# Linear attention and mixture of depths: key transposes in the state banks, a bank for the score row, and wider score compares

## The chip, the cores and the metric

The kernel runs on one core of one Trainium2 chip. The metric is device time in microseconds (us); the kernel before takes 194.52 us, the median of three runs. The engines of a core are PE (TensorE, the matrix engine; its weight loads are listed as PEld), DVE (VectorE), ACT (ScalarE), POOL (GpSimd) and SP (SyncE, used here for loads). The matrix engine writes to PSUM, which has eight banks per partition of 512 float32 values each.

## The reference

Two stages follow each other. The first is a block-wise linear attention with decay over 4 batches, 8 heads, 768 positions and head size 64, in blocks of 64:

```python
intra = einsum(einsum(qb, kb) * Dmask, vb)          # inside the block
inter = einsum(qb * lam_pow, kv_state)              # from the state
out[:, :, sl] = intra + inter
kv_state = lam_block * kv_state + einsum(kb * rev_pow, vb)
```

The second is a mixture of depths on the result x, reshaped to (4, 768, 512). A score x @ w_gate is taken for every token, the 128 tokens of a batch with the highest scores are chosen, and only these go through a two-layer network:

```python
xe = x[b, top_idx]
ye = maximum(xe @ w1, 0) @ w2                       # 512 -> 1024 -> 512
out[b, top_idx] = xe + sigmoid(score)[:, None] * ye
```

## The kernel before

A group g is 128 positions of one batch for all heads, that is two blocks of 64; there are NT = 6 groups per batch and NG = 24 in all. The main loop takes one step per group. The order of instructions on every engine is the order in which the program is written: nothing is reordered by a scheduler, and each engine works its instructions off in that order, waiting where an operand or a buffer isn't ready. The framework places the waits.

**PSUM.** Two output tiles `po` (two banks each) hold scores and outputs of a group. Two banks `pu` (one per block) hold the key-value products of a group, in their lower 256 columns. Two more banks, handed out in turn by `bank()`, serve everything else: the transposed queries `tp_qT` and keys `tp_kT`, and for the expert `pt` (its transposed input), `ph` (hidden layer), `py` (output) and `pk` (chosen tokens). While the expert holds a bank for `ph` or `py`, all others share the remaining one.

**A step g.** The steps of attention overlap: in step g, `from_scores(g)` (line 282) and `outputs(g)` finish group g; `scores(g+1)` (line 217), `from_states(g+1)` (line 271) and `masked(g+1)` (line 224, on DVE, writes `p`) work on the next one; `state_products(g+2)` (line 240) fills `pu`, and `next_state` (lines 259 and 261, on DVE) adds it to the state that `decay_state` (line 250, on POOL) has scaled. There are two states per group, and so two such pairs per step. `transposes(g+2)` brings queries and keys into the form that the matmuls need (line 195 on PE, copies in line 199 on ACT), `queries_decayed(g+2)` (line 204) and `keys_decayed(g+3)` (line 184) scale them on POOL. `gate_scores(g)` (line 306, on DVE) yields the score of each token.

**Choosing tokens.** `row(g-1)` transposes the scores of a group so that every partition has them in a row (line 326): it writes them into columns 256 to 383 of `pu[0]`, and ACT copies them to `sc_row` (line 329). `compare(g-1)` counts on DVE how many tokens beat each token: ties within the group (line 339), earlier groups against the new row, one instruction for each (line 345), and the new group against all so far (line 350). Both `pu` readers of a score row must be done before the next step's state products may use the bank. After a batch's last group `ranks` sums the counts, and `hit` (line 368) marks the token of each rank.

**The expert.** `plan(b)` lays its pieces out over the following steps. With s the first step after batch b: ranks run at the end of step s, `tokens` (line 379) early in step s+1, `fetch` gathers the rows from the output in memory with an indirect DMA (line 402, issued by POOL) at the start of step s+2, and `gate` (transposes of the gathered rows in line 412, and the gate's value) comes in step s+3 behind the attention's state products. Then follow 8 `hidden` pieces (line 440) and 8 `back` pieces (line 454), two or three per step, and a scatter (line 466). The last batch's expert and most of the one before run after the loop.

Of the kernel before, what the change touches and what calls it, by code (L numbers as in the profile page):

```python
# [8 lines left out]
FP32 = mybir.dt.float32  # L9
BF16 = mybir.dt.bfloat16  # L10
# [7 lines left out]
def kernel(  # L18
# [18 lines left out]
    L = 128  # L37
# [125 lines left out]
    def bank(shape, name, hold=False):  # L163

        tag = next(t for t in banks if t not in held)
        banks.remove(tag)
        banks.append(tag)
        if hold:
            held.append(tag)
        return ps_m.tile(shape, FP32, name=name, tag=tag)  # L170
# [17 lines left out]
        )  # L188
        kds[g] = kd

    def transposes(g, name, keep):
        t = loaded[g][0 if name == "qT" else 1]
        tp = bank([128, NHP, L], "tp_" + name)
        for hp in range(NHP):
            nc.tensor.transpose(  # L195
                tp[:, hp, :], in_=t[:, 2 * hp : 2 * hp + 2, :], identity=ident[:]
            )
        dst = att.tile([128, NHP, L], FP32, name=name)
        nc.scalar.copy(out=dst[:], in_=tp[:])  # L199
        keep[g] = dst  # L200

    def queries_decayed(g):
        qs = att.tile([128, NHP, L], FP32, name="qs")
# [27 lines left out]
    def start_u(g):  # L231
        us[g] = [ps_u.tile([128, 512], FP32, name=f"pu{c}") for c in range(2)]
# [80 lines left out]

        return out[0 : b + 1].flatten_outer_dims()

    rows_, beatens, toks, pbs = {}, {}, {}, {}

    def row(g, u, i=0):

        b, t = divmod(g, NT)  # L320
        if t == 0:
            rows_[b] = mod.tile([128, S], FP32, name="sc_row", tag="sc_row")
            beatens[b] = mod.tile([128, NT, NT + 1], FP32, name="beaten")
            nc.gpsimd.memset(beatens[b][:], 0.0)
        pb = us.pop(u)[i][:, 256 : 256 + L]
        nc.tensor.transpose(
            pb, in_=scs[b][:, t : t + 1].broadcast_to([128, 128]), identity=ident[:]
        )
        nc.scalar.copy(out=rows_[b][:, t * L : (t + 1) * L], in_=pb)  # L329
        pbs[g] = pb  # L330

    def compare(g):
        b, t = divmod(g, NT)
        sc, pb, beaten = scs[b], pbs.pop(g), beatens[b]
        cmp = mod.tile([128, S], BF16, name="cmp")
        nc.vector.scalar_tensor_tensor(  # L339
            out=cmp[:, :L], in0=pb, scalar=sc[:, t : t + 1], in1=not_before[:],  # L340
            op0=ALU.is_equal, op1=ALU.mult, accum_out=beaten[:, t, NT : NT + 1],
        )
        for n in range(t):
            cmp = mod.tile([128, S], BF16, name="cmp")
            nc.vector.tensor_scalar(  # L345
                out=cmp[:, :L], in0=pb, scalar1=sc[:, n : n + 1], scalar2=None,
                op0=ALU.is_gt, op1=ALU.add, accum_out=beaten[:, n, t : t + 1],
            )
        cmp = mod.tile([128, S], BF16, name="cmp")
        nc.vector.tensor_scalar(  # L350
            out=cmp[:, : (t + 1) * L], in0=rows_[b][:, : (t + 1) * L],
            scalar1=sc[:, t : t + 1], scalar2=None, op0=ALU.is_ge, op1=ALU.add,
            accum_out=beaten[:, t, t : t + 1],
        )

    def places(b):


        hits = []

        def ranks():
            rank = mod.tile([128, NT], FP32, name="rank")
            nc.vector.tensor_reduce(
                out=rank[:], in_=beatens[b][:], axis=mybir.AxisListType.X, op=ALU.add
            )
            for i in range(NGR):
                hit = mod.tile([128, NT, 128], BF16, name="hit")
                nc.vector.tensor_tensor(
                    out=hit[:], in0=rank[:].unsqueeze(2).broadcast_to([128, NT, 128]),
                    in1=token[:, i * 128 : (i + 1) * 128].unsqueeze(1).broadcast_to([128, NT, 128]),  # L370
                    op=ALU.is_equal,
                )
                hits.append(hit)

        def tokens():
            pk = bank([128, NGR, 2], "pk")
            for i in range(NGR):
                for t in range(NT):
                    nc.tensor.matmul(
                        pk[:, i, :], lhsT=hits[i][:, t, :], rhs=ids[:, b * NT + t, :],  # L380
                        start=(t == 0), stop=(t == NT - 1),
                    )
# [91 lines left out]

    early, gates, later, ranked = {}, {}, {}, {}
    busy_until = [0]

    def put(step, key, piece):  # L480
        later.setdefault(step, []).append((key, piece))

    def in_order(pieces):
        for _, piece in sorted(pieces, key=lambda kp: kp[0]):
            piece()

    def plan(b):
        last = b == B - 1
        s = (b + 1) * NT
        ranks, tokens = places(b)  # L490
        if last:

            def last_row():
                start_u(NG + 2)
                row(NG - 1, NG + 2, 1)
                compare(NG - 1)
                ranks()

            put(s, 35, last_row)
            put(s, 85, tokens)  # L500
        else:
            ranked[s] = ranks
            put(s + 1, 5, tokens)
        for i in range(NGR):
            s = max(s, busy_until[0])
            fetch, gate, pieces = expert(b, i)
            if s + 3 >= NG:
                s = max(s, NG)
                put(s, 86, fetch)
                put(s + 1, 0, gate)  # L510
                for j, piece in enumerate(pieces):
                    put(s + 2, j, piece)
                busy_until[0] = s + 3
                continue
            early.setdefault(s + 2, []).append(fetch)
            gates[s + 3] = gate

            whole = s + 9 <= NG
            counts = [2, 3, 3, 3, 3, 2] if whole else [1, 1, 2]
            assert len(pieces) == 16  # L520
            where = [(s + 3 + i, 10 * (j + 1)) for i, n in enumerate(counts) for j in range(n)]
            where = [w for w in where if w[0] < NG]
            where += [(NG, 10 * (j + 1)) for j in range(len(pieces) - len(where))]
            for (step, key), piece in zip(where, pieces):
                put(step, key, piece)
            busy_until[0] = s + 6 if whole else NG

    keys_decayed(0)
    transposes(0, "qT", qTs)
    transposes(0, "kT", kTs)  # L530
    queries_decayed(0)
    keys_decayed(1)
    start_u(0)
    state_products(0)
    next_state(0)
    decay_state(1)
# [1 line left out]
    decay_state(2)  # L538
    for g in range(3, AHEAD):
        load(g)  # L540
    transposes(1, "qT", qTs)
    transposes(1, "kT", kTs)
    queries_decayed(1)
    keys_decayed(2)
    scores(0)
    from_states(0)
    start_u(1)
    state_products(1)
    masked(0)
    next_state(2)  # L550
# [4 lines left out]
    for g in range(NG):  # L555
        if g + AHEAD < NG:
            load(g + AHEAD)
        if 0 <= g - NT + 2 < n_w:
            load_weights(g - NT + 2)
        if g + 2 < NG:  # L560
            decay_state(2 * g + 4)
        for piece in early.pop(g, []):
            piece()
        from_scores(g)
        outputs(g)
        if g + 1 < NG:
            scores(g + 1)
            from_states(g + 1)
            masked(g + 1)
        start_u(g + 2)  # L570
        if g + 2 < NG:
            state_products(g + 2)
            next_state(2 * g + 4)
            decay_state(2 * g + 5)
        gate_scores(g)
        if g + 2 < NG:
            next_state(2 * g + 5)
        pieces = later.pop(g, [])
        starts = g in gates
        if starts:  # L580
            gates.pop(g)()
        if g + 2 < NG:
            transposes(g + 2, "qT", qTs)
            queries_decayed(g + 2)
        if g + 3 < NG:
            keys_decayed(g + 3)
        if starts and g > 0:
            row(g - 1, g + 2)
            compare(g - 1)
        in_order(pieces)  # L590
        if g + 2 < NG:
            transposes(g + 2, "kT", kTs)
        if not starts and g > 0 and NGR:
            row(g - 1, g + 2)
            compare(g - 1)
        if g in ranked:
            ranked.pop(g)()
        if g % NT == NT - 1 and NGR:
            plan(g // NT)
# [35 lines left out]
```

## Time and profile before

| | |
|---|---|
| device time, median of 3 | 194.52 us |
| profiled execution, span | 192.9 us |
| PE busy | 157.5 us, 82% |
| DVE busy | 104.0 us, 54% |
| POOL busy | 98.9 us, 51% |
| ACT busy | 66.1 us, 34% |
| DMA traffic | 32.26 MB, of which the 16 engines are nine tenths busy until about 116 us |
| copies of qT and kT (ACT) | 24 of 584 ns, 24 of 587 ns |
| compares of line 345 (DVE) | 60, 17.8 us in all |
| gathers of expert rows | 4, of 3.4 to 6.5 us from issue to landing |

A busy share is a mean over the whole span. The program has stretches with different limits: a start, eight steps with attention alone, then steps in which the expert's matmuls fill the matrix engine, and an end with the expert alone. A line of the timeline begins with start and duration in us, then engine, source line, operation, output and inputs, sizes and count; in brackets follows how long the engine was idle before and what ended that. "issue" in such a bracket means that the profile shows no releasing instruction.

### The profile page before, as it was taken

The page shows a single profiled execution, that of the slowest core. Times are in us where ns is not written, and L with a number is a line of the kernel's source. Part 1 is how long each engine was busy: PE and PEld are TensorE (multiplying, and loading weights), DVE is VectorE, ACT ScalarE, POOL GpSimd, SP SyncE. Part 2 cuts the span into 40 slices and gives each one's busy share as a digit, 9 for nine tenths or more (in the row PEclk, how much of TensorE's full clock was granted, in tenths as well). Part 3 has the DMA queues.
Part 4 walks back from the last instruction along what each step waited for, and adds up shares of the span by engine and source line. Part 5 has one row for each costly group of instructions (what it writes and reads, how often), then busy time and mean ns, then how long its engine had stood idle before and what let it go on. Part 6 is the DMA issues. An engine that isn't in the chain of part 4 may idle for free.

```text
span 192.9 us, 8120 instructions
## 1 busy us (share of the span) xinstructions
PE 157.5 (82%) x3520; PEld 125.3 (65%) x3520; DVE 104.0 (54%) x393; ACT 66.1 (34%) x161; POOL 98.9 (51%) x110
## 2 busy tenths in 40 slices
PE   0896776969777399998888899989699899979980
PEld 0675665757666399896646689876467689439630
DVE  4824353667884653448664564754927678730010
ACT  2234333544443224533314353444234352111100
POOL 3486777476858641773556846458197410130002
PEclk9999998899999859999999999999999999999999
DMA  4999999998999999998999993110103211011001
GB/s 104 221 225 268 230 226 256 223 259 187 254 297 287 302 252 259 271 286 233 232 259 259 250 251 112 59 49 11 58 17 99 109 61 54 0 54 54 3 0 56
DMA packets 80964, 32.26 MB, mean 167 GB/s; under 512 B 75680, under 2 KB 75680, under 8 KB 80928
## 3 DMA queue, kind: packets, MB, share of 16 engines
q1 hardware_dynamic: 76688, 23.34, 54.2%
q10 hardware_dynamic: 3600, 6.30, 8.9%
q0 software_dynamic: 640, 2.10, 3.1%
q8 instruction: 28, 0.46, 0.9%
q14 instruction: 8, 0.07, 0.1%
HBM read 24.38 MB, written 7.34 MB: 164 GB/s over the span
## 4 chain that ended last, share of the span: by engine, by line
PE 51%; issue 16%; DVE 10%; POOL 9%; DMA 7%; ACT 4%; POOLq 1%; SPq 0%; ACTq 0%
PE ph L440 12%; PE py L454 11%; PE pu L240 5%; PE po L217 5%; PE po L271 5%; PE tp_qT L195 4%; PE tp_kT L195 4%; POOL qs L204 4%; DMA xs<-out_dram,tok 3%; PE po L282 3%; POOL kd L184 3%; POOL decayed L250 3%; DMA kn<-in_k_dram 3%; ACT kT L199 2%; DVE cmp L345 2%
## 5 line engine op out<-in xcount | busy, mean ns | idle before, releaser
L250 POOL TENSOR_TENSOR decayed<-state,decay 128x256 f32<-128x256 f32 x40 | 35.4, 884 | 39.0 <-DVE state L261 31.6
L204 POOL TENSOR_TENSOR qs<-qT,qpow 128x512 f32<-128x512 f32 x24 | 30.5, 1269 | 14.4 <-ACT qT L199 8.9
L440 PE MATMUL ph<-xsT,w_sb 128*128 128x128 f32 x256 | 32.6, 286 | 0.9 <-ACT xsT L416 0.7
L440 PEld LDWEIGHTS ph<-xsT,w_sb 128*128 128x128 f32 x256 | 31.2, 200 | 1.7 <-ACT xsT L416 1.5
L199 ACT COPY qT<-tp_qT 128x512 f32<-128x512 f32 x24 | 14.0, 584 | 50.0 <-PE tp_qT L195 46.8
L454 PE MATMUL py<-w_sb,hs 128*128 128x512 f32 x64 | 29.2, 596 | 0.0
L224 DVE TENSOR_TENSOR p<-po,mask 128x512 f32<-128x512 f32 x24 | 16.5, 689 | 19.2 <-PE po L271 19.2
L184 POOL TENSOR_TENSOR kd<-kn,kpow 128x512 f32<-128x512 f32 x24 | 25.1, 1044 | 3.2 <-DMA kn<-in_k_dram 3.1
L261 DVE TENSOR_TENSOR state<-pu,decayed 128x256 f32<-128x256 f32 x40 | 16.8, 421 | 16.9 <-POOL decayed L250 16.3
L240 PE MATMUL pu<-vn,kd 64*64 64x64 f32 x704 | 19.7, 229 | 7.3 <-issue 5.2
L240 PEld LDWEIGHTS pu<-vn,kd 64*64 64x64 f32 x704 | 16.1, 140 | 10.1 <-issue 7.0
L217 PE MATMUL po<-qT,kT 64*64 64x64 f32 x768 | 18.3, 228 | 5.0 <-issue 4.5
L271 PE MATMUL po<-state,qs 64*64 64x64 f32 x704 | 17.3, 225 | 5.9 <-POOL qs L204 3.0
L199 ACT COPY kT<-tp_kT 128x512 f32<-128x512 f32 x24 | 14.1, 587 | 23.3 <-PE tp_kT L195 23.3
L195 PE MATMUL tp_qT<-ident,qn 128*128 128x128 f32 x96 | 17.4, 309 | 5.1 <-DMA qn<-in_q_dram 5.1
L339 DVE SCALAR_TENSOR_TENSOR cmp<-pu,sc,not_before 128x128 bf16<-128x128 f32 x24 | 8.4, 349 | 23.8 <-ACT sc_row L329 17.0
L217 PEld LDWEIGHTS po<-qT,kT 64*64 64x64 f32 x768 | 14.5, 137 | 8.1 <-issue 5.4
L271 PEld LDWEIGHTS po<-state,qs 64*64 64x64 f32 x704 | 14.5, 138 | 7.1 <-POOL qs L204 3.7
L454 PEld LDWEIGHTS py<-w_sb,hs 128*128 128x128 f32 x64 | 11.5, 190 | 11.0 <-issue 11.0
L345 DVE TENSOR_SCALAR_CACHE_REDUCE cmp<-pu,sc 128x128 bf16<-128x128 f32 x60 | 17.8, 347 | 0.0
L298 ACT COPY x_b<-po 64x256 f32<-64x256 f32 x48 | 17.6, 366 | 0.6
L282 PE MATMUL po<-vn,p 64*64 64x64 f32 x768 | 16.8, 224 | 0.3 <-DVE p L224 0.3
(55 smaller groups left out, 170.6 us busy)
## 6 DMA issues: line engine op xcount, KB each, us to landing
qn<-in_q_dram SPq DMA_DIRECT2D x24, 256.0 KB, 5.3
kn<-in_k_dram SPq DMA_DIRECT2D x24, 256.0 KB, 5.5
vn<-in_v_dram SPq DMA_DIRECT2D x24, 256.0 KB, 6.0
out_dram<-x_b ACTq DMA_DIRECT2D x24, 256.0 KB, 3.6
w_sb<-in_moe_w_dram SPq DMA_DIRECT2D x8, 512.0 KB, 5.9
wg_b<-in_moe_w_gate_dram SPq DMA_DIRECT2D x1, 256.0 KB
xs<-out_dram,tok POOLq DMA_INDIRECT x4, 4.3
out_dram<-y,tok POOLq DMA_INDIRECT x4, 3.1
```

The costliest lines, as they stand in the source:

```text
L184: nc.gpsimd.tensor_tensor(out=kd[:], in0=loaded[g][1][:], in1=kpow[:].rearrange("p a b -> p (a b)").unsqueeze(2).broadcast_to([128, H, D]) ...
L195: nc.tensor.transpose(tp[:, hp, :], in_=t[:, 2 * hp : 2 * hp + 2, :], identity=ident[:])
L199: nc.scalar.copy(out=dst[:], in_=tp[:])
L204: nc.gpsimd.tensor_tensor(out=qs[:], in0=qTs[g][:], in1=qpow[:].rearrange("p a c i -> p a (c i)"), op=ALU.mult)
L217: nc.tensor.matmul(po[half[c], hh, 1, hp, :], lhsT=kT[half[hh], hp, half[c]], rhs=qT[half[hh], hp, half[c]], start=True, stop=True, skip_g ...
L240: nc.tensor.matmul(us[g][c][half[hh], hp * D : (hp + 1) * D], lhsT=kd[half[c], h, :], rhs=vn[half[c], h, :], start=True, stop=True, skip_g ...
L250: nc.gpsimd.tensor_tensor(out=t[:], in0=states[n][:], in1=decay[:], op=ALU.mult)
L271: nc.tensor.matmul(pos[g][half[hh ^ c], hh, 0, hp, :], lhsT=qs[half[hh], hp, half[c]], rhs=states[n][half[hh], hp, :], start=(hp == 0), st ...
L282: nc.tensor.matmul(pos[g][half[hh ^ c], hh, 0, hp, :], lhsT=p[half[c], hh, hp, :], rhs=vn[half[c], 2 * hp + hh, :], start=(hp == 0 and (2 ...
L345: nc.vector.tensor_scalar(out=cmp[:, :L], in0=pb, scalar1=sc[:, n : n + 1], scalar2=None, op0=ALU.is_gt, op1=ALU.add, accum_out=beaten[:, ...
L440: nc.tensor.matmul(ph[:, fc % 4, :], lhsT=w1_sb[:, dc, fc * 128 : (fc + 1) * 128], rhs=keep["xsT"][:, dc, :], start=(dc == 0), stop=(dc == ...
L454: nc.tensor.matmul(py[:], lhsT=keep["hs"][:, fc, :], rhs=w2_sb[:, fc, :], start=(fc == 0), stop=(fc == NFC - 1),)
```

## The change

The change does four things.

1. The transposed keys are written into columns 256 to 511 of the two `pu` banks, two head pairs in each, and copied out by two ACT instructions in place of one. Both transposes of a group now stand together, ahead of `next_state`, and only the queries take one of the two shared banks.
2. The score row takes a shared bank of its own (`pb`) and leaves `pu`.
3. Older groups are compared with newer ones for two or three groups at a time, from the copied row in SBUF.
4. The order is changed: in the start `queries_decayed(0)` comes ahead of `keys_decayed(0)`; `keys_decayed(g+3)` moves to the front of the step; `gate` moves ahead of the transposes; ranks run one step later; tokens and the gather move to the end of step s+2, while `gate` stays in step s+3; the pieces of the third expert start with one each in the last three steps; the last two rows of the loop come together in step NG-2.

It is meant to free the shared banks and the state banks earlier, and to take waits for compares and ranks away from the matrix engine.

```diff
-    def transposes(g, name, keep):
-        t = loaded[g][0 if name == "qT" else 1]
-        tp = bank([128, NHP, L], "tp_" + name)
...
+    def transposes(g):
+        tq = bank([128, NHP, L], "tq")
+        tk = [u[:, NHP * D :].rearrange("p (a i) -> p a i", i=L) for u in us[g]]
...
+        nc.scalar.copy(out=qT[:], in_=tq[:])
+        kT = att.tile([128, NHP, L], FP32, name="kT")
+        for i in range(2):
+            nc.scalar.copy(out=kT[:, i * W : (i + 1) * W, :], in_=tk[i])
...
-        pb = us.pop(u)[i][:, 256 : 256 + L]
+        pb = bank([128, L], "pb")
...
+    def count_later(b, groups, last):
+        for t in groups:
+            if upto[b][t] < last:
+                cols = slice((upto[b][t] + 1) * L, (last + 1) * L)
+                count(b, t, cols, ALU.is_gt, last)
+                upto[b][t] = last
...
     def compare(g):
-        for n in range(t):
-            cmp = mod.tile([128, S], BF16, name="cmp")
-            nc.vector.tensor_scalar(
-                out=cmp[:, :L], in0=pb, scalar1=sc[:, n : n + 1], scalar2=None,
-                op0=ALU.is_gt, op1=ALU.add, accum_out=beaten[:, n, t : t + 1],
-            )
...
+        count(b, t, slice(0, (t + 1) * L), ALU.is_ge, t)
+        if t == NT // 2 - 1 or (b == B - 1 and t == NT - 2):
+            count_later(b, range(t), t)
+        elif t == NT - 2:
+            count_later(b, range(NT // 3), t)
+        elif t == NT - 1:
+            count_later(b, range(NT // 3, NT - 2), t)
...
         def ranks():
+            count_later(b, range(NT), NT - 1)
...
-            ranked[s] = ranks
-            put(s + 1, 5, tokens)
+            ranked[s + 1] = ranks
+            put(s + 2, 15, tokens)
...
-            early.setdefault(s + 2, []).append(fetch)
+            put(s + 2, 16, fetch)
...
-            counts = [2, 3, 3, 3, 3, 2] if whole else [1, 1, 2]
+            counts = [2, 3, 3, 3, 3, 2] if whole else [1, 1, 1]
...
+    start_u(0)
+    transposes(0)
+    queries_decayed(0)
     keys_decayed(0)
-    transposes(0, "qT", qTs)
-    transposes(0, "kT", kTs)
-    queries_decayed(0)
     keys_decayed(1)
-    start_u(0)
...
-        for piece in early.pop(g, []):
-            piece()
+        if g + 3 < NG:
+            keys_decayed(g + 3)
...
             state_products(g + 2)
+        if g in gates:
+            gates.pop(g)()
+        if g + 2 < NG:
+            transposes(g + 2)
             next_state(2 * g + 4)
             decay_state(2 * g + 5)
...
+        for r in {NG - 2: [g - 1, g], NG - 1: []}.get(g, [g - 1]):
+            if r >= 0 and NGR:
+                row(r)
+                compare(r)
```

More of the change, by code (lines that the diff above doesn't have):

```diff
@@ L189, in keys_decayed @@
         kds[g] = kd
-    def transposes(g, name, keep):
-        t = loaded[g][0 if name == "qT" else 1]
-        tp = bank([128, NHP, L], "tp_" + name)
-        for hp in range(NHP):
-            nc.tensor.transpose(
-                tp[:, hp, :], in_=t[:, 2 * hp : 2 * hp + 2, :], identity=ident[:]
-            )
-        dst = att.tile([128, NHP, L], FP32, name=name)
-        nc.scalar.copy(out=dst[:], in_=tp[:])
-        keep[g] = dst
+    def transposes(g):
+        tq = bank([128, NHP, L], "tq")
+        tk = [u[:, NHP * D :].rearrange("p (a i) -> p a i", i=L) for u in us[g]]
+        W = NHP // 2
+        for i, dst in ((0, tq), (1, None)):
+            for hp in range(NHP):
+                nc.tensor.transpose(
+                    dst[:, hp, :] if i == 0 else tk[hp // W][:, hp % W, :],
+                    in_=loaded[g][i][:, 2 * hp : 2 * hp + 2, :], identity=ident[:],
+                )
+        qT = att.tile([128, NHP, L], FP32, name="qT")
+        nc.scalar.copy(out=qT[:], in_=tq[:])
+        kT = att.tile([128, NHP, L], FP32, name="kT")
+        for i in range(2):
+            nc.scalar.copy(out=kT[:, i * W : (i + 1) * W, :], in_=tk[i])
+        qTs[g], kTs[g] = qT, kT
     def queries_decayed(g):
@@ L314, in rows_upto, with row @@
         return out[0 : b + 1].flatten_outer_dims()
-    rows_, beatens, toks, pbs = {}, {}, {}, {}
-    def row(g, u, i=0):
+    rows_, beatens, toks, upto = {}, {}, {}, {}
+    def row(g):
         b, t = divmod(g, NT)
@@ L324, in row @@
             nc.gpsimd.memset(beatens[b][:], 0.0)
-        pb = us.pop(u)[i][:, 256 : 256 + L]
+            upto[b] = list(range(NT))
+        pb = bank([128, L], "pb")
         nc.tensor.transpose(
-            pb, in_=scs[b][:, t : t + 1].broadcast_to([128, 128]), identity=ident[:]
+            pb[:], in_=scs[b][:, t : t + 1].broadcast_to([128, 128]), identity=ident[:]
         )
-        nc.scalar.copy(out=rows_[b][:, t * L : (t + 1) * L], in_=pb)
-        pbs[g] = pb
+        nc.scalar.copy(out=rows_[b][:, t * L : (t + 1) * L], in_=pb[:])
@@ new lines, in row, with count @@
+        cmp = mod.tile([128, S], BF16, name="cmp")
+        nc.vector.scalar_tensor_tensor(
+            out=cmp[:, :L], in0=pb[:], scalar=scs[b][:, t : t + 1], in1=not_before[:],
+            op0=ALU.is_equal, op1=ALU.mult, accum_out=beatens[b][:, t, NT : NT + 1],
+        )
+    def count(b, t, cols, op, at):
+        cmp = mod.tile([128, S], BF16, name="cmp")
+        nc.vector.tensor_scalar(
+            out=cmp[:, : cols.stop - cols.start], in0=rows_[b][:, cols],
+            scalar1=scs[b][:, t : t + 1], scalar2=None, op0=op, op1=ALU.add,
+            accum_out=beatens[b][:, t, at : at + 1],
+        )
@@ L335, in compare @@
+    def count_later(b, groups, last):
[4 more added lines that the diff above has]
+                upto[b][t] = last
     def compare(g):
         b, t = divmod(g, NT)
-        sc, pb, beaten = scs[b], pbs.pop(g), beatens[b]
-        cmp = mod.tile([128, S], BF16, name="cmp")
[L339 to L342, printed above, removed]
@@ L343, in compare @@
-        for n in range(t):
-            cmp = mod.tile([128, S], BF16, name="cmp")
-            nc.vector.tensor_scalar(
-                out=cmp[:, :L], in0=pb, scalar1=sc[:, n : n + 1], scalar2=None,
-                op0=ALU.is_gt, op1=ALU.add, accum_out=beaten[:, n, t : t + 1],
[L348 to L354, printed above, removed]
+        count(b, t, slice(0, (t + 1) * L), ALU.is_ge, t)
@@ L356, in places, with compare_last @@
+        if t == NT // 2 - 1 or (b == B - 1 and t == NT - 2):
[4 more added lines that the diff above has]
+            count_later(b, range(NT // 3, NT - 2), t)
+    def compare_last():
+        b, t = B - 1, NT - 1
+        count(b, t, slice(t * L, (t + 1) * L), ALU.is_ge, t)
     def places(b):
@@ L471, in expert @@
         return fetch, gate, [hidden(f) for f in range(NFC)] + [back(f) for f in range(NFC)]
-    early, gates, later, ranked = {}, {}, {}, {}
+    gates, later, ranked = {}, {}, {}
     busy_until = [0]
@@ L493, in last_row @@
             def last_row():
-                start_u(NG + 2)
-                row(NG - 1, NG + 2, 1)
-                compare(NG - 1)
+                count(b, NT - 1, slice(0, (NT - 1) * L), ALU.is_ge, 0)
+                row(NG - 1)
+                compare_last()
                 ranks()
@@ L540 @@
         load(g)
-    transposes(1, "qT", qTs)
-    transposes(1, "kT", kTs)
+    start_u(1)
+    transposes(1)
     queries_decayed(1)
@@ L546 @@
     from_states(0)
-    start_u(1)
     state_products(1)
@@ L569 @@
             masked(g + 1)
-        start_u(g + 2)
         if g + 2 < NG:
+            start_u(g + 2)
             state_products(g + 2)
+        if g in gates:
+            gates.pop(g)()
+        if g + 2 < NG:
+            transposes(g + 2)
             next_state(2 * g + 4)
@@ L577 @@
             next_state(2 * g + 5)
[L578 to L583, printed above, removed]
-            queries_decayed(g + 2)
[L585 to L595, printed above, removed]
+            queries_decayed(g + 2)
+        in_order(later.pop(g, []))
+        for r in {NG - 2: [g - 1, g], NG - 1: []}.get(g, [g - 1]):
+            if r >= 0 and NGR:
+                row(r)
+                compare(r)
         if g in ranked:
```

## The prediction

> **What bounds the kernel now.** I read the page first: engine totals, then the clock row.
>
> ```profile
> span 192.9 us, 8120 instructions
> PE 157.5 (82%) x3520; PEld 125.3 (65%) x3520; DVE 104.0 (54%) x393; ACT 66.1 (34%) x161; POOL 98.9 (51%) x110
> PEclk9999998899999859999999999999999999999999
> ```
>
> PE leads, but 82% is a mean of two regimes. I call T_g the start of step g's first matmul (from_scores, line 282) in the timeline: T0 13.18, T1 18.25, T9 61.76, T10 73.58, T11 79.71, T12 86.20, T13 92.93, T14 101.11, T15 107.29, T16 114.23, T20 141.76, T22 154.49, T23 157.52. Up to step 8 there is no expert work and PE is half idle. Steps 10 to 22 carry expert matmuls and PE sets the pace. First the timeline of an early step:
>
> ```profile
> 45.04 1.11 POOL L250 TENSOR_TENSOR decayed<-state,decay 128x256 f32<-128x256 f32 x1 [1.50 <-DVE state L261]
> 46.11 1.27 POOL L204 TENSOR_TENSOR qs<-qT,qpow 128x512 f32<-128x512 f32 x1
> 47.35 1.04 POOL L184 TENSOR_TENSOR kd<-kn,kpow 128x512 f32<-128x512 f32 x1
> 47.44 0.69 PE L271 MATMUL po<-state,qs 64*64 64x64 f32 x32
> 48.44 0.69 PE L240 MATMUL pu<-vn,kd 64*64 64x64 f32 x32 [0.31 <-DMA vn<-in_v_dram]
> 49.06 0.66 PE L195 MATMUL tp_qT<-ident,qn 128*128 128x128 f32 x4
> 49.28 0.41 DVE L261 TENSOR_TENSOR state<-pu,decayed 128x256 f32<-128x256 f32 x1
> 49.78 1.11 POOL L250 TENSOR_TENSOR decayed<-state,decay 128x256 f32<-128x256 f32 x1 [0.71 <-DVE state L261]
> 49.81 0.59 ACT L199 COPY qT<-tp_qT 128x512 f32<-128x512 f32 x1 [2.50 <-PE tp_qT L195]
> 50.29 0.59 ACT L199 COPY kT<-tp_kT 128x512 f32<-128x512 f32 x1
> ```
>
> It is a loop over engines: decayed, qs (POOL), from_states and state products (PE), state (DVE), decayed again: 4.74 us here, 5.4 on average from T1 to T9 (43.5 over 8). The state starts beside the transposes and is long done when kT is copied.
>
> In the expert steps PE waits in two places, seen in the timeline:
>
> ```profile
> 88.13 0.35 DVE L345 TENSOR_SCALAR_CACHE_REDUCE cmp<-pu,sc 128x128 bf16<-128x128 f32 x1
> 88.59 0.69 PE L240 MATMUL pu<-vn,kd 64*64 64x64 f32 x32 [0.54 <-issue]
> 97.64 0.30 PE L379 MATMUL pk<-ids,hit 128*128 128x2 bf16 x6 [0.83 <-DVE hit L368]
> ```
>
> State products start 0.1 us after the last compare that reads the score row out of pu ("issue" hides the bank's release), and the token matmuls wait for hit. Third, the gather of the expert's rows before step 9, and what followed:
>
> ```profile
> 60.99 1.15 POOL L402 DMA_INDIRECT xs<-out_dram,tok  x1 [0.77 <-DVE p L224]
> 67.61 1.08 PE L412 MATMUL pt<-ident,xs 128*128 128x128 f32 x4 [1.75 <-DMA xs<-out_dram,tok]
> 68.49 1.06 PE L195 MATMUL tp_qT<-ident,qn 128*128 128x128 f32 x4
> 69.56 3.62 PE L440 MATMUL ph<-xsT,w_sb 128*128 128x128 f32 x16
> ```
>
> The gather took 6.5 us, PE waited, and then 16 matmuls took 3.62 us where 2.05 is usual: the slow clock (5 in the clock row). The list of gathers gives 3.4, 4.3, 6.5 as shortest, median and longest.
>
> **What the Trainium skill says.** "PSUM — Partial Sum Buffer", section "PSUM bank collisions raise a hardware error": two engines on one bank and quadrant collide, reads against reads included, whatever the columns, so they must be ordered by bank. The trace agrees:
>
> ```profile
> DVE cmp L339 <- ACT sc_row L329: 17.0, 15, 2.3
> 56.12 0.13 PEld L326 LDWEIGHTS pu<-ident,sc 128*128 128x128 f32 x1 [0.37 <-DVE state L261]
> ```
>
> The first (list of waits) is one reader of pu waiting for another, the second (timeline) a write to pu's upper columns waiting for a read of its lower ones. Same page, "Engine vs sequencer instructions": ScalarE, VectorE and GpSimd queues are strict FIFO and matmuls keep program order; a late operand therefore holds all behind it, as at 67.61. "TensorE: Matmul & The Clock Gate", "What's actually happening": after an idle window of about 3.4 us the clock halves. Here a 1.75 us wait in a thin stretch was enough. "SBUF — State Buffer", "Who interferes with whom": a VectorE instruction with two SBUF inputs contends with GpSimd's reads; decayed takes 1.11 us beside gate_scores and 0.73 elsewhere.
>
> **The change, part by part.**
>
> *Keys into the state banks.* Eight transposes as before; one 0.59 us copy becomes two of 256 columns (0.37 by the x_b row), 0.15 us on an ACT 34% busy: nothing. But next_state, now emitted behind the transposes, reads a bank that PE writes (kT) and ACT reads (kT copy) first, and must wait for both. Loop from the start of qs: 1.33 to from_states, 0.47 for it, 0.62 for the products (2.42); 0.75 until ACT starts qT (49.06 to 49.81), 0.48 until kT, 0.37 for half a kT, 0.04, state 0.42, 0.07, decayed 1.07 to the next qs: 5.62. Unobstructed, the old loop without 0.75+0.48+0.37 and with state behind p is about 4.2; it measured 5.4 with its fetch stalls and compares. Behind the waiting state on DVE are gate_scores and the second state, and decayed and qs on POOL wait for them.
>
> *Order at the start.* qs(0) goes ahead of kd(0) on POOL. qs(0) can't begin before 8.43 (qpow), so kd(0), which ended at 7.4, runs 9.7 to 10.7, and kd(1) to 11.8. Products(0) move from 7.46 to 10.8; then state 12.4, decayed 13.2, second state 13.7, upper-bank kT of group 1 14.3, scores and from_states at the slow clock 15.6, p 16.4: T0 16.4 (+3.2).
>
> *Early steps.* Following the loop, T1 = 19.9, first qs at 22.1, T2 = 25.7, then 5.62 a step; step 3 prepares a batch's last group, has no second decayed, and takes 3.7. T9 = 63.4 with token matmuls (0.25), +1.6. Fetch stalls of 0.5 to 1.7 us ("issue" inside matmul groups) and slow clock in the longer gaps: 0 to 5, I take +1.5.
>
> *Gather.* Tokens and gather move to the end of step s+2, behind qs on POOL; gate still needs xs in step s+3, and PE meets it ahead of all transposes. Step 8: qs starts at 65.2, gather at 65.2+1.27+0.16 = 66.65, landed at 6.48 later 73.1; pt to T10 took 5.97 before, so T10 = 79.1 against 73.58: +5.5, of which 1.6 came with T9. Step 14: products end at T14+2.35, qs starts 5.55, gather 6.98, landed (4.3) 11.28, while PE was there at 7.9. Then pt, tq, tk 1.5, two hidden pieces 1.8, row 0.2 make 14.75, with a slow clock (3.4 us at half speed cost 1.7) 16.45; T14 to T16 was 13.12: +3.3. Step 20: gather 3.6 (the last one's), landed 10.58, one piece: 13.2, slow 14.5; was 12.73: +1.7.
>
> *Score row in its own bank, fewer compares.* Products no longer wait for compares, tokens no longer for hit: the four steps T10 to T14 took 27.53, and four unhindered ones (T16 to T17, 6.13) take 24.5: -3.0, twice -6.0. Compares: per batch 15 at 0.27 become 9 of 128 to 384 columns, 4.05 to 3.2 us on DVE, hidden as DVE has slack; the is-equal and is-ge ones stay. kd earlier removes waits of 0.3 us on a loop that is now another's: nothing.
>
> *End.* Row(22) in step 22 waits for its gate score: T22 to T23 3.4 against 3.03 (+0.4). From T23 to the last gather's use, 14.4 becomes 13.9, as five pieces instead of four cover it: -0.5. After that nothing changes.
>
> Sum: +5.5 +3.3 +1.7 -6.0 +0.4 -0.5 = +4.4, with 1.5 for stalls and clock +5.9: 194.5 to 200.4.
>
> **Rivals.**
> A, even (0.22): gathers land in 4.3 at step 9 (-2.2), no slow clock at 15 and 21 (-3.0): 195 to 196. For it: loads thin out as PE stalls; against: DMA is 9 tenths busy until 116 us.
> B, faster (0.15): the state read isn't held by the kT copy, loop about 4.9 (-4.9 over seven steps), and A's savings: about 189. Against: the 17.0 us of reader behind reader.
> C, slower still (0.13): the early loop's 2 us gap ahead of from_states keeps the clock low; slow products and transposes add 1.4 to half the steps or more: 204 to 206. For it: the fall at 32 us after a 1.73 us gap; against: similar gaps at 15 and 41 had none.
>
> **How the numbers follow.** My forecast (0.50) is the sum, 200.4. C and nearly all of it lie over 198.4 (+2%): slower 0.60; A and the lower edge of the forecast are within 2%: 0.25; B: 0.15. Low 192 leaves out most of B, high 206 the worst of C; between are the bounds of gather (3.4 to 6.5) and stalls (0 to 5).
>
> **What would show it.** Right: T0 near 16.4; early steps near 5.6 with state waiting for kT's ACT copy and from_states for qs; pt waiting for the gather 2 to 5 us three times; products waiting for no compare; steps 10 to 13 at 6.1. Wrong: state starting beside the transposes, or xs landed before PE reaches the gate.

## The result, and the profile after

The changed kernel takes 204.39 us (median of four runs, 201.98 to 205.06); the kernel before, in the same series, 195.03. The ratio is 1.047 with a 95% interval of 1.032 to 1.062: slower. The forecast was 200.4 with a range of 192 to 206. Here and below, a ratio with an interval is of the runs within 1.5% of each kernel's fastest; medians and ranges are of all runs.

First the page of the kernel after, by the same lines as before.

```profile
span 202.5 us, 8090 instructions
PE 155.7 (77%) x3520; PEld 127.8 (63%) x3520; DVE 104.9 (52%) x351; ACT 68.2 (34%) x185; POOL 100.2 (49%) x110
PEclk9999996669996995999999975999999999999998
```

The busy times hardly moved (PE 157.5 to 155.7, POOL 98.9 to 100.2). The loss is therefore waiting, in a span that grew by 9.6 us. The clock row reads 6 from 30 to 46 us, 6 again from 61 to 66 us, and 7 and 5 from 116 to 127 us, where the row of before reads 8 or 9.

The starts of the steps, T_g as the prediction defines them, say where it went. The next table sets the differences of both traces beside the prediction's terms.

| stretch | before | after | measured | predicted |
|---|---|---|---|---|
| to T0 | 13.18 | 16.71 | +3.5 | +3.2 |
| T0 to T9 | 48.58 | 53.92 | +5.3 | -1.6, and +1.5 for stalls |
| T9 to T10 (first gate) | 11.82 | 13.11 | +1.3 | +3.9 |
| T10 to T14 | 27.53 | 24.80 | -2.7 | -3.0 |
| T14 to T16 (second gate) | 13.12 | 18.39 | +5.3 | +3.3 |
| T16 to T20 | 27.53 | 23.15 | -4.4 | -3.0 |
| T20 to T22 (third gate) | 12.73 | 13.39 | +0.7 | +1.7 |
| T22 to T23 | 3.03 | 5.00 | +2.0 | +0.4 |
| T23 to the last gather's use | 14.38 | 13.30 | -1.1 | -0.5 |

The measured terms add up to +9.9, the predicted ones to +5.9. Now the timeline of the kernel after, the first state products and then an early step; the columns are as in the lines of before.

```profile
10.31 1.13 PE L247 MATMUL pu<-vn,kd 64*64 64x64 f32 x32 [3.33 <-POOL kd L184]
...
27.79 0.42 DVE L268 TENSOR_TENSOR state<-pu,decayed 128x256 f32<-128x256 f32 x1 [1.38 <-ACT kT L206]
28.29 1.10 POOL L257 TENSOR_TENSOR decayed<-state,decay 128x256 f32<-128x256 f32 x1 [1.87 <-DVE state L268]
29.36 1.26 POOL L211 TENSOR_TENSOR qs<-qT,qpow 128x512 f32<-128x512 f32 x1
...
30.68 1.13 PE L278 MATMUL po<-state,qs 64*64 64x64 f32 x32 [2.20 <-POOL qs L211]
31.58 1.08 PE L247 MATMUL pu<-vn,kd 64*64 64x64 f32 x32
...
33.80 0.59 ACT L203 COPY qT<-tq 128x512 f32<-128x512 f32 x1 [4.63 <-PE tq L198]
34.28 0.65 ACT L206 COPY kT<-pu 128x256 f32<-128x256 f32 x2
34.76 0.42 DVE L268 TENSOR_TENSOR state<-pu,decayed 128x256 f32<-128x256 f32 x1 [2.19 <-ACT kT L206]
```

Read the chain from one state (27.79) to the next (34.76). The state starts decayed, that lets qs start on POOL, qs releases from_states after 2.20 us of waiting, the state products follow, then the transposes, the copies of qT and kT, and only then the next state, which waited 2.19 us for the kT copy out of its bank. In this round from_states, products and transposes took 1.13, 1.08 and 1.11 us where 0.69, 0.65 and 0.66 are usual. Such rounds are the steps of 7.2, 7.3 and 7.0 us (steps 2, 3 and 7); steps 5 and 6 took 5.61 and 5.68. The list of waits of the kernel after shows the totals: the wait's name, its sum, how often, the longest.

```profile
DVE state L268 <- ACT kT L206: 17.7, 15, 2.2
PE po L278 <- POOL qs L211: 15.9, 8, 2.2
PE pt L434 <- DMA xs<-out_dram,tok: 8.1, 3, 4.1
PE pb L334 <- DVE tok_f L407: 2.5, 2, 1.2
```

In the list of before, compares that waited for the row's copy stood at 17.0 us; they are at 5.6 us now. The new first line lies on the loop that paces the early steps. The last line is a new wait that the prediction does not have: in the expert's steps the score row and the chosen tokens share the one bank left. The gathers and the end, again from the timeline of the kernel after:

```profile
73.48 1.15 POOL L424 DMA_INDIRECT xs<-out_dram,tok  x1 [0.16 <-DVE cmp L350]
...
79.09 1.09 PE L434 MATMUL pt<-ident,xs 128*128 128x128 f32 x4 [4.12 <-DMA xs<-out_dram,tok]
...
115.65 1.00 POOL L424 DMA_INDIRECT xs<-out_dram,tok  x1 [0.15 <-DVE y L484]
121.19 1.09 PE L434 MATMUL pt<-ident,xs 128*128 128x128 f32 x4 [2.87 <-DMA xs<-out_dram,tok]
...
160.97 0.63 PE L434 MATMUL pt<-ident,xs 128*128 128x128 f32 x4 [1.13 <-DMA xs<-out_dram,tok]
...
167.81 0.08 DVE L313 DVE_READ_ACCUMULATOR2_ANT sc<- 128x1 f32 x1
167.81 0.34 DVE L340 SCALAR_TENSOR_TENSOR cmp<-pb,sc,not_before 128x128 bf16<-128x128 f32 x1
168.22 0.32 PE L334 MATMUL pb<-ident,sc 128*128 128x128 f32 x1 [1.63 <-DVE cmp L340]
```

The gather was issued at 60.99 before and at 73.48 now; PE reached its rows 4.12 us before they landed, and everything after them on PE waited with them.

### The profile page after: what moved, and what is told of

Read it like the earlier page. It is cut to its first block, busy times and chain, and to the rows that moved or that the text cites. A ratio compares the mean times of both kernels' runs of the same rounds, so it can differ in the third digit from the quotient of the medians.

```text
span 202.5 us, 8090 instructions
## 1 busy us (share of the span) xinstructions
PE 155.7 (77%) x3520; PEld 127.8 (63%) x3520; DVE 104.9 (52%) x351; ACT 68.2 (34%) x185; POOL 100.2 (49%) x110
## 4 chain that ended last, share of the span: by engine, by line
PE 45%; POOL 16%; issue 13%; DMA 10%; DVE 9%; ACT 4%; POOLq 1%; DVEq 0%; ACTq 0%
PE ph L462 10%; POOL decayed L257 8%; DMA xs<-out_dram,tok 7%; PE tq L198 6%; PE py L476 6%; PE po L278 6%; PE pu L247 6%; POOL qs L211 5%; PE po L289 4%; PE po L224 3%; PE pu L198 3%; DVE state L268 3%; ACT qT L203 3%; POOL kd L184 2%; DMA lam_b<-in_lam_dram 2%
## 5 line engine op out<-in xcount | busy, mean ns | idle before, releaser
L257 POOL TENSOR_TENSOR decayed<-state,decay 128x256 f32<-128x256 f32 x40 | 35.7, 894 | 44.8 <-DVE state L268 33.2
L211 POOL TENSOR_TENSOR qs<-qT,qpow 128x512 f32<-128x512 f32 x24 | 30.5, 1269 | 12.4 <-ACT qT L203 7.5
L268 DVE TENSOR_TENSOR state<-pu,decayed 128x256 f32<-128x256 f32 x40 | 17.0, 424 | 31.4 <-ACT kT L206 17.7
L278 PE MATMUL po<-state,qs 64*64 64x64 f32 x704 | 18.5, 236 | 17.1 <-POOL qs L211 15.9
L203 ACT COPY qT<-tq 128x512 f32<-128x512 f32 x24 | 14.1, 586 | 48.0 <-PE tq L198 48.0
L350 DVE TENSOR_SCALAR_CACHE_REDUCE cmp<-sc_row,sc 128x128 bf16<-128x128 f32 (+5 forms) x63 | 29.5, 513 | 0.0
L278 PEld LDWEIGHTS po<-state,qs 64*64 64x64 f32 x704 | 15.7, 148 | 18.6 <-POOL qs L211 17.2
L184 POOL TENSOR_TENSOR kd<-kn,kpow 128x512 f32<-128x512 f32 x24 | 25.8, 1078 | 0.0
L198 PE MATMUL tq<-ident,qn 128*128 128x128 f32 x96 | 18.8, 328 | 4.8 <-DMA qn<-in_q_dram 4.8
L313 DVE CUSTOM_DVE_ANT_0 xg<-x_b,wg_b 128x512 f32<-128x512 f32 x24 | 20.3, 846 | 0.0
L198 PE MATMUL pu<-ident,kn 128*128 128x128 f32 x96 | 17.8, 314 | 0.4 <-DVE state L268 0.4
L305 ACT COPY x_b<-po 64x256 f32<-64x256 f32 x48 | 17.7, 368 | 0.6
L289 PEld LDWEIGHTS po<-vn,p 64*64 64x64 f32 x768 | 14.0, 140 | 5.6 <-issue 4.0
L289 PE MATMUL po<-vn,p 64*64 64x64 f32 x768 | 17.4, 230 | 0.1
```

The costliest lines, as they stand in the source:

```text
L184: nc.gpsimd.tensor_tensor(out=kd[:], in0=loaded[g][1][:], in1=kpow[:].rearrange("p a b -> p (a b)").unsqueeze(2).broadcast_to([128, H, D]) ...
L198: nc.tensor.transpose(dst[:, hp, :] if i == 0 else tk[hp // W][:, hp % W, :], in_=loaded[g][i][:, 2 * hp : 2 * hp + 2, :], identity=ident[:],)
L211: nc.gpsimd.tensor_tensor(out=qs[:], in0=qTs[g][:], in1=qpow[:].rearrange("p a c i -> p a (c i)"), op=ALU.mult)
L257: nc.gpsimd.tensor_tensor(out=t[:], in0=states[n][:], in1=decay[:], op=ALU.mult)
L268: nc.vector.tensor_tensor(out=new[:], in0=u, in1=decayed.pop(n)[:], op=ALU.add)
L278: nc.tensor.matmul(pos[g][half[hh ^ c], hh, 0, hp, :], lhsT=qs[half[hh], hp, half[c]], rhs=states[n][half[hh], hp, :], start=(hp == 0), st ...
```

## The experiments

All are timed beside the kernel before, whose medians in the four series were 195.74, 194.43, 194.28 and 195.48 us. "After" is the changed kernel. Only some of the comparisons came with an interval; the others are given as median and range. The theory is that the late gather and the key copy in the state's bank cost more than freed compares bring back.

**The start's order alone.** Edit against after:

```diff
     transposes(0)
-    queries_decayed(0)
     keys_decayed(0)
+    queries_decayed(0)
     keys_decayed(1)
```

> The changed kernel, but in the start keys are decayed ahead of queries, as before. Theory (three losses: start order, state read held by the key copies, late gather): the first step begins near 13.3 us instead of 16.7, and the time falls by about 3.3 to 201. Rival (the start is hidden, since early steps wait for loads anyway): within 1 us of the changed kernel, 204.

203.53 us (202.94 to 205.06), a gain of 0.9: the rival's size, though not by its reason. Two lines of its timeline:

```profile
12.01 0.69 PE L198 MATMUL pu<-ident,kn 128*128 128x128 f32 x2 [1.51 <-DVE state L268]
19.85 0.33 PE L278 MATMUL po<-state,qs 64*64 64x64 f32 x3 [2.10 <-issue]
```

The products of group 0 came back to 7.5 us, but the keys of group 1 now wait for the state that reads the other half of their bank, and a stall follows for which the trace shows no releaser (the last section says what it is). T0 is 15.40, 1.3 earlier, and T9 is 69.91 against 70.63. With the bank shared as it is, the order at the start is worth little.

**The keys back in one shared bank, in all steps.** Edit against after:

```diff
-        tk = [u[:, NHP * D :].rearrange("p (a i) -> p a i", i=L) for u in us[g]]
+        tkb = bank([128, NHP, L], "tk")
...
+        tk = [tkb[:, :W, :], tkb[:, W:, :]]
...
-        for i in range(2):
-            nc.scalar.copy(out=kT[:, i * W : (i + 1) * W, :], in_=tk[i])
+        nc.scalar.copy(out=kT[:], in_=tkb[:])
```

> The changed kernel, but the transposed keys go to a shared bank and are copied out by one instruction; order unchanged. Theory (state read held by the key copies): the state no longer waits for the key copy, early steps fall from 6.2 us on average (49.4 over eight) to about 4.5 without slow-clock stretches, step 9 begins near 54; in expert steps the keys wait for the query copy in the one free bank, some 0.7 us in each of about 13 steps, +9. Net: 195 to 200. Rival (the early loop is set by the earlier decay of keys on POOL, or by loads): early steps stay near 6 us and the time rises above 208.

202.44 us (201.13 to 203.53), 2.0 less and short of what was expected. Its list of waits:

```profile
PE po L278 <- POOL qs L211: 0.9, 2, 0.6
PE tk L199 <- ACT qT L204: 5.8, 8, 0.7
```

The first line was 15.9 us: with the state free of the kT copy, the early loop is gone, and T1 to T9 took 43.6 us against 49.4 (43.5 before the change). At T10 the kernel was 5.3 us ahead of after. In the expert's steps, though, keys and queries take turns at the one bank left (second line); T16 to T22 took 41.3 us against 36.5, and at T22 the lead was gone. So the state banks are the wrong place for the keys in the early steps and the right one in the late ones. The expectation had both halves. The late one cost 5.6 us from T10 to T22, where 9 was expected; the early one brought less than expected, step 9 beginning at 65.28 and not near 54. Seven stalls like this one stand between T1 and T9:

```profile
61.72 0.50 PE L224 MATMUL po<-qT,kT 64*64 64x64 f32 x18 [2.13 <-issue]
```

They come to 7.95 us. Without them, by an estimate that takes them off in full, the eight steps would have taken 35.7 us, which is the 4.5 a step that was expected.

**The gather one step earlier.** Edit against after:

```diff
-            ranked[s + 1] = ranks
-            put(s + 2, 15, tokens)
+            ranked[s] = ranks
+            put(s + 1, 15, tokens)
...
-            put(s + 2, 16, fetch)
+            put(s + 1, 16, fetch)
```

> The changed kernel, but ranks, tokens and gather come one step earlier, so that the gather has a whole step before its use. Theory: the waits for the gather (4.1, 2.9 and 1.1 us) go, with them the slow clock behind the first two (1 to 2 us each), 9 us less: near 195. Rival (PE's wait for the gather only takes the place of another wait): at most 3 us less, over 201.

193.99 us (191.32 to 196.15): 10.4 less, and level with the kernel before (195.74, 190.87 to 197.47). The first gather and its use in this kernel's timeline:

```profile
67.64 1.15 POOL L424 DMA_INDIRECT xs<-out_dram,tok  x1 [1.86 <-issue]
...
74.97 1.11 PE L434 MATMUL pt<-ident,xs 128*128 128x128 f32 x4
```

No matmul waits for xs. T9 is 70.27, as in after, so nothing came from the early steps; T10 is 79.72 instead of 83.74, T16 116.50 instead of 126.93. The late gather is the largest single cost of the change.

**Wide compares alone.** Edit against the kernel before; the row stays in the state's bank:

```diff
-        for n in range(t):
-            cmp = mod.tile([128, S], BF16, name="cmp")
-            nc.vector.tensor_scalar(
-                out=cmp[:, :L], in0=pb, scalar1=sc[:, n : n + 1], scalar2=None,
...
+        if t == NT // 2 - 1 or (b == B - 1 and t == NT - 2):
+            count_later(b, range(t), t)
```

> The kernel before with one part of the change: compares with newer groups two or three at a time, from the copied row; the score row stays in the state bank, so only the tie compare reads it there. Theory (this part is a gain): state products wait no longer for the compares (0.3, 0.55, 0.8 us in three steps of each of two batches, 3.3 us), and the time falls to 190 to 192. Rival (wide compares cost as much as they save, or the order of DVE work behind them matters more): 194 to 197.

192.04 us (190.54 to 193.04), within what was expected: the median is 3.7 below that of the kernel before. The ranges overlap (before 190.87 to 197.47) and there is no interval for this pair, so the gain is likely, but not shown. The state products wait for a compare only once, 0.8 us. But hit is ready later, and PE waits for it in three steps (5.6 us). The next kernel tries to step around this.

**Wide compares, and the tokens later in the step.** Edit against the one just told:

```diff
-            put(s + 1, 5, tokens)
+            put(s + 1, 35, tokens)
```

> The kernel before with the wide compares, and the token matmuls behind the three expert pieces of their step instead of ahead of them. Theory: with wide compares alone the token matmuls waited 2.2 us for hit, as three compares moved in front of the ranks; behind the pieces they find it ready, 4 us less in two batches: 188 to 189. Rival (the wait for tok takes its place, at the key transposes that share the bank): 191 to 193.

193.46 us (191.13 to 195.2): a little over the rival's range, with the wait that the rival named. From its list of waits:

```profile
PE tp_kT L195 <- DVE tok_f L397: 4.3, 2, 2.2
```

The wait for hit became one of the key transposes for tok_f in the shared bank. No gain shows.

**The late gather alone, in the kernel before.**

```diff
-            ranked[s] = ranks
-            put(s + 1, 5, tokens)
+            ranked[s + 1] = ranks
+            put(s + 2, 15, tokens)
...
-            early.setdefault(s + 2, []).append(fetch)
+            put(s + 2, 16, fetch)
```

> The kernel before with one part of the change: ranks one step later, tokens and gather at the end of the step before the gate, behind the decayed queries on POOL. Theory (the late gather is the largest loss of the change): PE waits 2 to 4 us for the gather at steps 9, 15 and 21 with a slow clock behind, less 1.5 us that the token matmuls no longer wait for hit: 6 to 9 us slower, 201 to 205. Rival (the gather was lost only because the gate stands ahead of the transposes in the changed kernel): within 3 us of before.

208.37 us (207.36 to 211.2), ratio 1.070 with an interval of 1.061 to 1.079. The direction was expected, the size (+14) was not. In its list of waits pt waits 12.4 us in all for the gathers. The timeline around the second one shows the rest:

```profile
115.99 1.12 PE L412 MATMUL pt<-ident,xs 128*128 128x128 f32 x4 [3.79 <-DMA xs<-out_dram,tok]
116.78 1.00 POOL L466 DMA_INDIRECT out_dram<-y,tok  x1 [4.93 <-DMA xs<-out_dram,tok]
...
118.58 0.42 DVE L261 TENSOR_TENSOR state<-pu,decayed 128x256 f32<-128x256 f32 x1 [6.09 <-POOL decayed L250]
```

The scatter of the expert before stands on POOL behind the gather and waits 4.93 us until that has landed. decayed stands behind the scatter, and so DVE stood idle for 6.09 us before the state. The Trainium skill, "PSUM — Partial Sum Buffer", section "Engine vs sequencer instructions", says that GpSimd's queue is strictly first in, first out; the trace agrees, by these 6.09 us. A late gather thus holds PE by its rows and, through POOL, the attention's states too. In the kernel after it is so as well: behind the second gather POOL waits 5.26 us at the scatter, put down to the gate's value, which is computed from the gathered rows, and decayed follows:

```profile
121.90 1.00 POOL L488 DMA_INDIRECT out_dram<-y,tok  x1 [5.26 <-DVE g L443]
122.93 0.73 POOL L257 TENSOR_TENSOR decayed<-state,decay 128x256 f32<-128x256 f32 x1
```

**Is the slow clock a cause of its own?** Edit against after, with added work: seven unread 128x128 matmuls in each of steps 0 to 8, to fill PE's wait for qs.

```diff
             scores(g + 1)
+            if g < 9:
+                warm()
             from_states(g + 1)
```

> The changed kernel with seven matmuls of the identity, whose result nobody reads, in each of steps 0 to 8 between scores and from_states: about 1.5 us of work in PE's gap of 2.2 us there. Theory (the gap lets the clock fall, and the slow products and transposes lengthen the loop: steps 2, 3 and 7 took 7.0 to 7.3 us where others took 5.6): all eight steps at 5.6 to 5.9, step 9 begins 3 to 4 us earlier, time about 201. Rival (the loop is long for another reason and the clock only follows): no less than 203.5.

206.89 us (205.53 to 210.05), ratio 1.061 with an interval of 1.051 to 1.070: no gain in time, and the expectation was missed. The time is as the rival had it, but the early steps did shorten, which the rival did not have. Its timeline:

```profile
28.81 1.83 PE L212 MATMUL warm<-ident 128*128 128x128 f32 x14
30.88 0.69 PE L283 MATMUL po<-state,qs 64*64 64x64 f32 x32 [0.24 <-POOL qs L216]
31.40 0.65 PE L252 MATMUL pu<-vn,kd 64*64 64x64 f32 x32
...
65.92 0.27 PE L229 MATMUL po<-qT,kT 64*64 64x64 f32 x1 [2.26 <-issue]
...
80.50 1.09 PE L439 MATMUL pt<-ident,xs 128*128 128x128 f32 x4 [5.78 <-DMA xs<-out_dram,tok]
```

With 1.83 us of filling, from_states and products are back at 0.69 and 0.65 us, and steps 1 to 3 take 5.75, 5.70 and 5.71 us where two of them took 7.2 and 7.3. So the loop itself is 5.7 us long at full clock, and the rest of those steps was the clock. The 2.9 us gained by T4 were gone by T9 (70.61 against 70.63): steps 4 to 7 together took 0.9 us more than in after, and step 8 took 8.21 us, with a stall of 2.26 us that has no releaser in the trace. The gather after it landed late as well, and step 11 has one more such stall, of 3.11 us. The filling changed more than the clock, so the time of this kernel does not price the clock alone; the comparison of steps 2 and 3 does.

**Three parts put right together.** The earlier gather, the start's order, and the keys of groups 0 to 10 in a shared bank, of later groups in the state banks:

```diff
+        shared = g < 11
+        if shared:
+            tkb = bank([128, NHP, L], "tk")
...
+        if shared:
+            nc.scalar.copy(out=kT[:], in_=tkb[:])
```

> The changed kernel with ranks, tokens and gather a step earlier, keys decayed ahead of queries in the start, and the keys of groups 0 to 10, which meet no expert work, in a shared bank with one copy; groups from 11 on use the state banks. Theory: the gain of the earlier gather alone (194.0) and that of shared banks in the first nine steps (5 us) add up, with 1 to 2 us of the start: 187 to 189, faster than both kernels. Rival (the early steps have slack behind the loads, so that a faster front part only waits later): 192 to 194.

188.03 us (186.62 to 191.75), ratio to the kernel before 0.964 with an interval of 0.955 to 0.972: as expected, and faster than both kernels. T0 is 12.95, T9 60.22. New in its list are waits for loads:

```profile
POOL kd L184 <- DMA kn<-in_k_dram: 9.6, 6, 3.2
PE ph L469 <- DMA w_sb<-in_moe_w_dram: 5.5, 2, 4.7
```

**The combined version less one part each.** First with the keys left in the state banks throughout (shared = False), then with the changed kernel's order at the start.

> The changed kernel with the gather of expert rows one step earlier and keys_decayed(0) ahead of queries_decayed(0); keys stay in the state banks. The gather alone gave 194.0. If the start's gain is kept once the gather is out of the way: T0 near 15.4 or less and 191 to 192.5. Rival: the late T0 is absorbed by the loads and by the state that waits for the keys' copy in the early steps, T9 stays at 69.5 to 70.5 and the time at 193.5 to 195. Keys in the state banks then are what is left of the loss against the combined version's 188.0.

> The changed kernel with the gather one step earlier and the keys of groups 0 to 10 in a shared bank; the start's order stays as changed. If the start's order is worth its T0 (about 3 us) in the combined version: 190.5 to 191.5. If loads set T9 and T10 in the combined version (expert weights in step 9, keys for kd), T9 near 63, T10 within 1 us of 73.7 and 188 to 189.5: then the start's order costs nothing of its own and all of the early loss is the keys' bank.

The first gave 192.5 to 201.1 us in four runs, which decides nothing. The second gave 190.93 (187.75 to 193.21). By its median this is near the value expected if the start's order is worth its own 3 us, 2.9 more than the combined version of the series before; but that version's range (186.62 to 191.75) overlaps. T9 was 62.38, near the other value, but two profiles of the combined version, this one and the one told next, have it at 60.22 and 62.89, so it decides nothing. The price of the start's order stays open. The first was then run longer, beside the combined version:

> The same kernel as the one with the earlier gather and the start's order, keys in the state banks: its four times spread from 192.5 to 201.1, and the profile was of the slowest. With more rounds: if the spread is the matrix engine's clock in the early steps (a 2 us gap ahead of from_states and then state products of 1.09 us instead of 0.7), the profile shows early steps of 5.6 to 5.7 us where the products take 0.7 us, and of 6.9 to 7.0 where they take 1.09, and the median lies between 192.5 and 197. Rival: the spread is the chip's and hits the kernel before alike: then its times spread as widely.

> The combined version (gather one step earlier, start's order, keys of groups 0 to 10 in a shared bank) beside the one that differs from it in the keys' bank alone, on the same chip. If the keys' bank in the early steps is what is left: 186.5 to 189, faster than the other by 5 us or more, and no step with state products at 1.09 us before step 9. Rival: keys cost little once the gather is earlier: within 2.5 us of the other.

With the keys in the state banks 192.88 us (189.3 to 197.6, 19 runs; ratio to the kernel before 0.984, interval 0.978 to 0.990), with those of groups 0 to 10 in a shared bank 188.16 (185.22 to 190.31, 6 runs). The difference of 4.7 us is well over the 2.5 that the rival allowed and a little under the 5 expected; two early steps of the combined version still had slow products, where none was expected. In the profile of the version with the keys in the state banks, the two state products below went with steps of 6.76 and 5.53 us, as expected of the clock:

```profile
27.33 1.08 PE L254 MATMUL pu<-vn,kd 64*64 64x64 f32 x32
...
33.90 0.65 PE L254 MATMUL pu<-vn,kd 64*64 64x64 f32 x32
```

Its times spread over 8.3 us, those of the kernel before in this series over 5.7 (192.62 to 198.35), so only part of the spread is its own.

## Why the prediction was right, and where it was not

The side (slower) and the mechanisms held; the size was 4.0 us short, within the range.

*The loop over engines* was right. The forecast was 5.62 us a step; undisturbed steps took 5.61 to 5.75, in after and with filled gaps, and the two named waits (state for the kT copy, from_states for qs) stand at 17.7 and 15.9 us. The edit that takes the kT copy out of the state's bank brings the second down to 0.9 us and brings T1 to T9 back to 43.6.

*"Fetch stalls ... and slow clock in the longer gaps: 0 to 5, I take +1.5"* is the term that failed most. T0 to T9 cost 6.9 us more than the loop's -1.6, and above its upper bound. Steps 2, 3 and 7 alone, at 7.20, 7.26 and 7.04 us, hold 4.6 of it over 5.62 each, and step 0, with a stall of 1.07 us without a releaser, another 1.1; the filled version shows for steps 2 and 3 that this is the clock. The step called short (3: no second decayed) was in effect step 4, at 4.32 instead of 3.7. Rival C, which gave this term 204 to 206, named the right cause and got the time, in part by luck. It assumed half the steps or more; in the profile it was three of nine. T0 to T9 came 5.4 over its -0.1, and all other terms together 1.4 below theirs.

*Start*: +3.2 predicted, +3.5 measured, products at 10.31 where 10.8 was worked out. Its price in the end is not that: 0.9 us came back when it was put right alone, and 1.1 beside the earlier gather (192.88 against 193.99, in different series). Where the keys are put right too, the medians give 2.9, which is not settled.

*Gather*: the three waits of 4.12, 2.87 and 1.13 us answer to "2 to 5 us three times", except that the last is shorter. The terms were shared out wrongly. The first step was dearer in the forecast by 2.6: the rows landed 5.6 us after the issue, not 6.48, and T10 came 4.65 us after them, not 5.97, where the slow clock (75.0 to 81.8 us in the trace) had already begun during the wait. T14 to T16 cost 2.0 more, as the rows landed 5.5 us after their issue, not 4.3, with 0.6 more behind them. T20 to T22 cost 1.0 less, as the clock did not fall there. In step 14, the score row's wait of 1.23 us for tok_f was on no list of mine; it lies ahead of the wait for the rows, so it cost little of its own. The sum, 7.3 against 8.9, understates what the late gather costs, since the kernel before waits for its gathers too (1.75 us at 67.61). With the gather put back, no matmul waits for rows, and the three stretches take 13.4 us less than in after; 2.5 of this is lost again in T10 to T14 and T16 to T20, and the time falls by 10.4.

*Compares*: -6.0 predicted, -7.1 measured, with steps 16 to 19 at 5.74 to 5.85 instead of 6.13. Wide compares in the kernel before bring 3.7 by the medians, as the row still shares the state's bank and tokens wait for hit there.

*End*: T22 to T23 +2.0, predicted +0.4. It was taken for a wait for the gate's score. That score was in fact ready only at 167.89; the trace names the compare of the row before, in the bank that both rows share, which ended last, at 168.15 (1.63 us of waiting). So the wait was the right one for the most part, and its length was not. T23 to the gather's use was -1.1 instead of -0.5.

Rivals A and B are out, though the clock stayed up at the third gather as A had it. The kernel came level with before only where the gather was put back, and the state never started ahead of the kT copy where they share a bank.

The stalls without a releaser (2.10 us, 2.26 us), which took much of the early gains of two experiments, are read in the last section. What stays open is the price of the start's order in the end. Whether the state could go ahead of the key transposes without serializing them the other way round wasn't tried.

## What to carry to other kernels

Before a tile moves into the free half of a bank, ask who reads the other half and whether that reader is on the loop that sets the pace: here the halves shared no data, and a copy of 0.37 us each held a state that everything else followed. The same move was right in steps where another engine was the bound, so it can be made by stage. When a transfer's issue moves one step later while its use stays, its wait is paid by everything queued behind the use, and the gains made elsewhere may not show until it is moved back.

## What the runs showed of the hardware

The clock fell with gaps of about 2 us, and not each time. Two lines of the timeline after, the first of which stands above too:

```profile
30.68 1.13 PE L278 MATMUL po<-state,qs 64*64 64x64 f32 x32 [2.20 <-POOL qs L211]
...
55.06 0.69 PE L278 MATMUL po<-state,qs 64*64 64x64 f32 x32 [2.20 <-POOL qs L211]
```

The same wait of 2.20 us ahead of the same 32 matmuls left them at 1.13 us once and at 0.69 the other time. The Trainium skill, "TensorE: Matmul & The Clock Gate", section "What's actually happening", puts the fall after an idle window of about 3.4 us; here shorter gaps, one in every step, were enough, and with 1.83 us of matmuls in them steps 1 to 3 kept the full clock.

The traces show what differs. In all 14 the granted clock changes only on a grid of 3.41 us. The next lines give stretches of that grid in the kernel after: from and to, length, PE's busy time, the granted clock, and two columns on the DMA.

```profile
27.21:30.62 3.41, 1.27 (x65) 1.00 0.95 213
30.62:34.04 3.42, 3.36 (x71) 0.50 1.12 279
51.10:54.52 3.42, 1.76 (x70) 1.00 0.90 241
54.52:57.93 3.41, 2.87 (x111) 1.00 1.16 297
```

The gap before 30.68 lies in one stretch, with PE idle for 2.14 us of it, and the next stretch has half the clock. The gap before 55.06 is divided by the tick at 54.52; PE is idle for 1.66 us of the first stretch and 0.54 us of the second, and the clock stays. Over the 14 traces, all 25 stretches at full clock with 2.05 to 2.92 us idle were followed by a slow one, none of the 569 with less than 1.48 us, and 28 of the 58 between. So it is not the length of a gap alone that counts, but how much idle time falls into one stretch of the grid. What decides between 1.48 and 2.05 us is open.

The stalls of PE without a releaser can be read too. The page has a DMA queue for instructions, here of the kernel after (packets, MB, share):

```profile
q8 instruction: 27, 0.44, 1.0%
```

The traces time each of its packets, of 16 KB. PE has 46 stalls of 1 us or more without a releaser in the 14 traces. Each ended 1.2 to 1.7 us after one of these packets had landed, and each stopped PE at a place in its order of instructions that comes back every 256 of them. With packets and places paired in order, PE passed such places 369 times, and never sooner than 1.0 us after the packet. So these were waits for PE's own instructions. The filled kernel has more of them, so the same places fall elsewhere in its steps.

Added matmuls can bring back the clock and still not pay: in steps 1 to 3 they cost no step time, in steps 5 and 6 about 0.3 us each (5.95 and 5.97 against 5.61 and 5.68), and the kernel took 206.89 us against 204.39.
